# Linear attention and a routed expert layer on one core: early weights' low halves on VectorE, six PSUM banks for the early region, region 1's splits behind the rest's, eight groups

## The chip, the core and the metric

The kernel runs on one core of a Trainium2 chip. Each core has five engines that work side by side from their own instruction streams: TensorE (PE, with its weight loads as PEld), VectorE (DVE), ScalarE (ACT), GpSimd (POOL) and SyncE (SP), which here only issues transfers. They share SBUF, an on-chip memory of 128 partitions, and PSUM, in eight banks of which TensorE writes its results. An engine runs its instructions strictly in the order in which they were written. It waits on semaphores that other engines and transfers raise.

The metric is the time of one execution on the device in microseconds (us). Three runs of the kernel before took 570.96, 573.08 and 573.12 us (median 573.08). The profile was taken in an execution of 571.51 us, of which 569.8 us lie between the first and the last instruction; all times of steps below count from that first instruction.

A difference between two kernels is told as a ratio of their times with a 95% interval.

## What is computed

A linear attention feeds a mixture of 16 experts. Every token gets the one expert that two argmax choices pick, and its output is weighted by both softmax shares.

```python
kv  = einsum('bhsd,bhse->bhde', k, v)              # 8 batches, 8 heads, 576 tokens, 64 dims
out = einsum('bhsd,bhde->bhse', q, kv)
x   = out / sqrt(mean(out * out, -1) + 1e-6) * g_norm   # -> 4608 tokens x 512
g_idx = argmax(x @ w_group)                        # 4 groups
e_idx = argmax(x @ w_expert[g_idx])                # 4 experts of that group
h   = relu(x @ w1[g_idx, e_idx])                   # 512 -> 1024
y   = softmax_share_g * softmax_share_e * (h @ w2[g_idx, e_idx])   # 1024 -> 512
```

All inputs and the output are fp32. The expert products are made in three terms: a number is split into a high part that the reduced format fp32r holds and a low part that is the rest, and high x high, high x low and low x high are added up in PSUM. So every weight half and every activation needs one instruction for its high part (ACT, `whi`, `hh`, `hhi`, `xh`) and one for its low part (`wlo`, `hl`, `hlo`, `xl`).

## The kernel before

**Stage 1, to about 125 us.** The attention's batches are read, multiplied and normalised in 36 tiles of 128 tokens. The tiles are taken in seven groups (`GS = [6, 5, 5, 4, 4, 6, 6]`). For each group VectorE works out the routing (maximum L717, exponentials L721, the chosen expert L736, the tokens' ranks by expert L769, their row numbers `keys` L789), and POOL puts each tile's rows at those numbers into a table in device memory (`put_rows`, L248). The order of all this is not written out. Each piece is a `step` with an engine, an estimated length, a rank and the steps it needs, and `give_out` lists them: on the engine that can start first it takes, of the steps that are ready, the one with the smallest rank. The ranks come from the tables `RANK`, `ROUTE`, `FOLD`, `LOADS`, `QLOADS`, `KVS`. A step's `take` and `give` count slots of a pool of 11 weight-sized buffers (`big`, tag `w8`).

**Early products.** The table's rows are sorted by expert into regions, the largest regions first. After group `EARLY = 4` the first 256 rows (`HEAD`) of one expert's region are already there. They are read (L271, `xq0`), turned (L1166) and multiplied by that expert's weights while the last groups are still being routed: layer 1 in plain fp32 in eight pieces of 128 columns (L321), each followed by its high part on ACT (`hhi` L1190) and its low part on VectorE (`hlo` L1194); layer 2 in three terms (L332, L333, L337) for three of its four quarters. The quarters are (row half, column half): (0,0), (1,0), (0,1). `early_bank` hands out PSUM, two banks in turn. `LOWS = 'GGDD'` puts the low parts of the first two weight quarters on POOL and those of the other two on VectorE (`split_low`, L232). The result goes to the buffer `yos`, which takes a slot of the pool.

**Handover.** From here on the order is as written in the code. SP reads region 0's remaining 128 rows (`read(0)`, L271) once all rows are put, then region 1's first weight half, region 1's 364 rows (`read(1)`, eight transfers, L268) and the other three weight halves (L205). TensorE does the fourth quarter of the early layer 2 (first `CUT = 3` pieces, then the turning of the 128 rows L1415, then the rest), the 128 rows' layer 1 (L1454, eight chunks of which are named `hf` 0 and 1), the turning of its result (`turn`, L1436) and its layer 2 (`rest_layer2`: L332, L333, L337). ACT makes `hr` (L1455) and the high parts `hT` (L1439), VectorE the low parts (L1440). POOL scatters `yos` into the output (L286) in two halves, with the scaling of region 1's rows (L293) between them.

Into this stretch fall region 1's own preparations: the splits of its first weight half in two quarters (`split_piece`: ACT L228, VectorE L232) and, four times, a block of its rows turned on VectorE (L283), split high on ACT (L1356) and low on VectorE (L1360).

**Regions 1 to 15** follow one another: layer 1 in eight pieces (TensorE L332, L333, L337; ACT `hh` L296; VectorE `hl` L297), layer 2, the way back to token order and the scatter (L1369), while the next region's weights are loaded and split. After that comes a short part for tokens over a region's capacity, which with these inputs has nothing to do.

Of the kernel before, what the change touches and what calls it, by code (L numbers as in the profile page):

```python
# [9 lines left out]
F32 = mybir.dt.float32  # L10
# [14 lines left out]
GS = [6, 5, 5, 4, 4, 6, 6]  # L25
XO = 20
XR = 18
QUICK = [0, 1, 2, 3, 4, 5, 6]
# [7 lines left out]
RANK = {'hl': 9.65, 'wh': 6.62, 'wd': 2136.43, 'ek': 25.19, 'o': 25.25, 'ok': -55.65, 'sq': 5942.05, 'red': 15.18, 'w': 4025.37, 'wl': 3910.86, 'wl2': 2990.79, 'xt': -40.19, 'xs': -2498.44, 'l1': -61.45, 'hs': -2328.8, 'l2': -1.69, 'lk': -39.03}  # L36
ROUTE = [30.82, 25.75, 32.74, 13.04, -1952.63, 21.42, -2905.74]
FOLD = [-322.89, 2985.26, -27.49, -32.52, -3125.23, -19.02, 8.4]
LOADS = [-10693.24, -8621.11, -104.17, -10.74, 24.09, 22.45, 18.56, 2987.32]
QLOADS = [-6674.02, -5.16, 6.84, 24.17, -12.07, 23.8, 24.74, 3747.92]  # L40
KVS = [-5947.45, 47.59, 752.46, 9.1, -13.16, 2244.94, -6.35, 6.78]
# [3 lines left out]
LOWS = 'GGDD'  # L45
FILL = 0.28
LG = 0.19
FQ = [0, 1, 2, 3, 4, 5, 6]
# [11 lines left out]
def tile_linattn_moe(ctx: ExitStack, tc: tile.TileContext, qm, qt, k, v, router, w1, w2, out):  # L60
# [304 lines left out]
    with ExitStack() as ph:  # L365
# [774 lines left out]
        def early_products(wt):  # L1140
# [35 lines left out]
            hs = []  # L1176
            for f_ in range(FC):
                def f(f_=f_):
                    if f_ == 0:
# [4 lines left out]
                s = step("PE", 1.75, r0 + RANK["l1"] + 0.1 * f_, x + [free.pop(0), wt[f_ // 4]], f,  # L1184
                         give=1 if f_ == FC - 1 else 0)
# [5 lines left out]
                s = step("A", 0.3, r0 + RANK["hs"] + 0.1 * f_, [s], f, take=2 if f_ == 0 else 0)  # L1191
# [4 lines left out]
                hs.append(step("D", 0.33, r0 + RANK["hl"] + 0.1 * f_, [s], f))  # L1196
# [3 lines left out]
            for p in range(4):  # L1200
                def f(p=p):
                    if p % 2 == 0:
                        st["ws"][2 + p // 2] = [st["ws"][2 + p // 2], None, None]
                    split_high(st["ws"][2 + p // 2], p % 2)
                s = step("A", 0.95, r0 + RANK["wh"] + 0.1 * p, [wt[2 + p // 2]], f, take=2 - 2 * (p % 2))
# [456 lines left out]
```

## Time and profile before

| | before |
|---|---|
| median of three runs | 573.08 us (570.96 to 573.12) |
| profiled execution | 571.51 us |
| its span, first to last instruction | 569.8 us |
| granted TensorE clock, mean | 0.990 |
| PE busy / DVE / ACT / POOL | 538.4 / 392.7 / 273.9 / 266.0 us |
| bytes moved, mean rate | 126.29 MB, 222 GB/s |
| early layer 2 begins (L332) | 125.46 us |
| region 0's last 128 rows, layer 1 begins (L1454) | 138.73 us |
| region 1's layer 1 begins (L332) | 164.98 us |
| region 1's first `hh` (L296) | 168.89 us |

How to read it: a row of the timeline has the start of a group of like instructions, the time that they span, engine, line, operation, output and inputs with their shapes, and how many there are. A bracket at the end has the engine's idle time just before, and what released it. A row of the windows has a stretch, its length, the busy time of each engine, the granted clock, the mean busy share of the 16 transfer engines, and GB/s.

### The profile page before, as it was taken

How to read it: one execution, taken by the hardware profiler on the slowest of the kernel's cores; microseconds unless marked ns; L12 is line 12 of the kernel's file. 1: busy time of each engine (PE TensorE's matmuls, PEld its weight loads, DVE VectorE, ACT ScalarE, POOL GpSimd, SP SyncE). 2: the span in 40 equal slices, each digit the busy share in tenths (PEclk: the TensorE clock that was granted, in tenths of full speed). 3: DMA queues.
4: the chain of work that ended last, by engine and by line, in shares of the span. 5: the costliest groups of instructions: out<-in, count | busy, mean ns of one | idle time of the engine just before them, and what ended most of it. 6: DMA issues, size and time to landing. Idle time of an engine off the chain costs nothing. (4 is left out here: it accounts for less than half of the span.)

```text
span 569.8 us, 11665 instructions
## 1 busy us (share of the span) xinstructions
PE 538.4 (94%) x4267; PEld 512.4 (90%) x4273; DVE 392.7 (69%) x813; ACT 273.9 (48%) x490; POOL 266.0 (47%) x278
## 2 busy tenths in 40 slices
PE   6899999879399999999999999999999999999995
PEld 3789888667189999999999999999999999999995
DVE  2249799781249787687768686778787777777760
ACT  0458777521245353444544545454545546555450
POOL 5003465662210273555555647383836537364271
PEclk9999999999889999999999999999999999999999
DMA  8999997928845738262847372837466473854010
GB/s 264 371 413 372 398 420 308 353 91 237 272 174 187 296 87 310 76 251 88 267 167 275 117 302 86 307 110 301 165 242 226 161 312 92 326 187 168 14 36 32
DMA packets 44462, 126.29 MB, mean 222 GB/s; under 512 B 6901, under 2 KB 26857, under 8 KB 33396
## 3 DMA queue, kind: packets, MB, share of 16 engines
q1 hardware_dynamic: 36468, 106.01, 51.6%
q0 software_dynamic: 7792, 19.48, 9.2%
q8 instruction: 34, 0.56, 0.4%
q10 hardware_dynamic: 144, 0.04, 0.1%
q14 instruction: 24, 0.20, 0.1%
HBM read 106.04 MB, written 20.58 MB: 222 GB/s over the span
## 5 line engine op out<-in xcount | busy, mean ns | idle before, releaser
L1369 POOL DMA_INDIRECT out_dram<-z,idx x141 | 168.1, 1192 | 167.3 <-DVE idx L1342 128.6
L332 PE MATMUL ps<-xh,whi 128*128 128x364 f32 (+14 forms) x480 | 144.1, 300 | 0.5 <-ACT xh L1356 0.5
L333 PE MATMUL ps<-xl,whi 128*128 128x364 f32 (+14 forms) x480 | 144.0, 300 | 0.4 <-DVE xl L1360 0.4
L337 PE MATMUL ps<-xh,wlo 128*128 128x364 f32 (+14 forms) x480 | 144.0, 300 | 0.0
L337 PE MATMUL psy<-hh,w2l 128*128 128x364 f32 (+13 forms) x448 | 135.1, 302 | 0.4 <-DVE w2l L310 0.4
L333 PE MATMUL psy<-hl,w2h 128*128 128x364 f32 (+13 forms) x448 | 135.5, 302 | 0.0
L332 PE MATMUL psy<-hh,w2h 128*128 128x364 f32 (+13 forms) x448 | 134.8, 301 | 0.0
L232 DVE TENSOR_TENSOR wlo<-wr,whi 128x1024 fp32r<-128x1024 f32 x62 | 94.8, 1530 | 39.0 <-ACT whi L228 22.8
L333 PEld LDWEIGHTS ps<-xl,whi 128*128 128x128 f32 x480 | 90.6, 189 | 0.9 <-DVE xl L1360 0.9
L332 PEld LDWEIGHTS ps<-xh,whi 128*128 128x128 f32 x480 | 90.6, 189 | 0.8 <-ACT xh L1356 0.8
L337 PEld LDWEIGHTS ps<-xh,wlo 128*128 128x128 f32 x480 | 90.5, 189 | 0.0
L296 ACT ACTIVATE hh<-ps 128x364 fp32r<-128x364 f32 (+14 forms) x120 | 50.6, 421 | 81.1 <-PE ps L337 79.6
L310 DVE TENSOR_TENSOR w2l<-wr,w2h 128x1024 fp32r<-128x1024 f32 x60 | 73.5, 1224 | 17.7 <-ACT w2h L306 17.5
L337 PEld LDWEIGHTS psy<-hh,w2l 128*128 128x128 f32 x448 | 84.5, 189 | 0.7 <-DVE w2l L310 0.7
L306 ACT CAST w2h<-wr 128x1024 fp32r<-128x1024 f32 x60 | 62.6, 1043 | 46.0 <-PE psy L333 46.0
L332 PEld LDWEIGHTS psy<-hh,w2h 128*128 128x128 f32 x448 | 84.5, 189 | 0.0
L333 PEld LDWEIGHTS psy<-hl,w2h 128*128 128x128 f32 x448 | 84.5, 189 | 0.0
L297 DVE SCALAR_TENSOR_TENSOR hl<-ps,hh 128x364 fp32r<-128x364 f32 (+14 forms) x120 | 55.6, 464 | 26.6 <-ACT hh L296 26.4
L248 POOL DMA_INDIRECT xs<-xo,keys x36 | 37.6, 1045 | 72.7 <-ACT y L683 42.2
L228 ACT CAST whi<-wr 128x1024 fp32r<-128x1024 f32 x64 | 66.3, 1037 | 4.2 <-PE ps L1454 3.1
L1356 ACT ACTIVATE xh<-xt,rw 128x364 fp32r<-128x364 f32 (+14 forms) x60 | 32.7, 545 | 70.7 <-DVE xt L283 70.7
L293 POOL TENSOR_TENSOR xq<-xq 128x1280 f32<-128x1280 f32 (+4 forms) x15 | 36.2, 2415 | 23.3 <-DMA xq<-xs 23.1
(272 smaller groups left out, 676.6 us busy)
## 6 DMA issues: line engine op xcount, KB each, us to landing
wr<-in_w_dram SPq DMA_DIRECT2D x64, 1024.0 KB
m_q<-in_qm_dram SPq DMA_DIRECT2D x8, 1024.0 KB
m_k<-in_k_dram SPq DMA_DIRECT2D x7, 1024.0 KB
m_v<-in_v_dram SPq DMA_DIRECT2D x7, 1024.0 KB
xq<-xs SPq DMA_DIRECT2D x24, 136.0 KB
xq<-xs SPq DMA_DIRECT2D x20, 153.0 KB
out_dram<-z,idx POOLq DMA_INDIRECT x141, 3.0
xq<-xs SPq DMA_DIRECT2D x8, 187.0 KB
```

The costliest lines, as they stand in the source:

```text
L228: nc.scalar.copy(out=hi, in_=w)
L232: eng.tensor_tensor(out=lo, in0=w, in1=hi.bitcast(F32), op=ALU.subtract)
L248: sc = nc.gpsimd.indirect_dma_start(out=xs, out_offset=bass.IndirectOffsetOnAxis(ap=keys[:, c:c + 1], axis=0), in_=x.rearrange("p i f -> p ...
L293: eng.tensor_tensor(out=part(x, n), in0=part(x, n), in1=factors(x, n), op=ALU.mult)
L296: nc.scalar.activation(out=hh, in_=ps, func=AF.Relu)
L297: nc.vector.scalar_tensor_tensor(out=hl, in0=ps, scalar=0.0, in1=hh.bitcast(F32), op0=ALU.max, op1=ALU.subtract)
L306: nc.scalar.copy(out=piece(hi, hf, i2), in_=halfpiece(wt[hf][0], i2))
L310: nc.vector.tensor_tensor(out=piece(lo, hf, i2), in0=halfpiece(wt[hf][0], i2), in1=piece(hi, hf, i2).bitcast(F32), op=ALU.subtract)
L332: nc.tensor.matmul(ps, lhsT=stat_h(c), rhs=mov_h(c), start=(c == 0), stop=False)
L333: nc.tensor.matmul(ps, lhsT=stat_h(c), rhs=mov_l(c), start=False, stop=False)
L337: nc.tensor.matmul(ps, lhsT=stat_l(d), rhs=mov_h(d), start=False, stop=(d == n - 1))
L1369: sc = nc.gpsimd.indirect_dma_start(out=out4, out_offset=bass.IndirectOffsetOnAxis(ap=idx[:, g:g + 1], axis=0), in_=z[:, g, :], in_offset= ...
```

## The change

Five things are changed.

1. The 36 tiles are taken in eight groups instead of seven, the last two of 4 and 2 tiles in place of 6, and all tables of ranks hold other numbers. Attention work and its loads keep their number and their sizes.
2. All four early low halves are made on VectorE, behind the last group's ranks (`kr`); `LOWS` is gone.
3. `early_bank` hands out six banks in turn: the two of before and the four of the attention's output (`ps_o`, two tiles of two banks).
4. The early layer 2 is made by passes: for (0,0) and (1,0) first all 16 high x high products, then the 16 of high weights with low activations, then the 16 of low weights; then the same for (0,1). It has 72 matmuls as before. Its result goes into the first half of the `xx` buffer, which is free by then, so that `yos` takes no slot.
5. In the handover SP reads region 1's rows ahead of its first weight half; each of the other three weight halves is issued behind a piece of TensorE's work; and the two splits of the first half stand behind the two `turn`s instead of ahead of the first.

```diff
-GS = [6, 5, 5, 4, 4, 6, 6]
+GS = [6, 5, 5, 4, 4, 6, 4, 2]
-RANK = {'hl': 9.65, 'wh': 6.62, 'wd': 2136.43, ...}
+RANK = {'hl': 36.17, 'wh': 5.91, 'wd': 107.42, ...}
...
-LOWS = 'GGDD'
...
             def early_bank(nm):
+                i = bank[0] % 6
                 bank[0] += 1
-                return (ps_k, ps_e)[(bank[0] - 1) % 2].tile([P, 512], F32, name=nm, tag=("psk", "pse")[(bank[0] - 1) % 2])
+                if i < 2:
+                    return (ps_k, ps_e)[i].tile([P, 512], F32, name=nm, tag=("psk", "pse")[i])
+                if i % 2 == 0:
+                    t["o"] = ps_o.tile([P, 2, 512], F32, name=nm, tag="pso")
+                return t["o"][:, i % 2]
-            free = [done["kk", B - 1], None]
+            free = [done["kk", B - 1], None] + [done["lk", NTL - 2 + i // 2] for i in range(4)]
...
-                s = step(LOWS[p], 1.4 if LOWS[p] == "D" else 2.3, r0 + RANK["wd"] + 0.1 * p, [s] + ([done["kr", len(groups) - 1]] if p > 1 else []),
-                         lambda p=p: split_low(st["ws"][2 + p // 2], p % 2, nc.vector if LOWS[p] == "D" else nc.gpsimd),
+                s = step("D", 1.24, r0 + RANK["wd"] + 0.1 * p, [s, done["kr", len(groups) - 1]],
+                         lambda p=p: split_low(st["ws"][2 + p // 2], p % 2, nc.vector),
...
-            for n, (j, hf) in enumerate(((0, 0), (1, 0), (0, 1))):
+            def passes(j, hf, x):
+                js = slice(j * P, (j + 1) * P)
+                h, w = (t["h"], t["h"], t["l"])[x], st["ws"][2 + hf][(1, 2, 1)[x]]
+                for c in range(FC):
+                    nc.tensor.matmul(t["l2", j, hf][:, 0:DM // 2], lhsT=h[:, c, js], rhs=w[:, c, :],
+                                     start=(x == 0 and c == 0), stop=(x == 1 and c == FC - 1))
+            at = {}
+            for n, (j, hf, x) in enumerate([(j, 0, x) for x in (0, 2, 1) for j in range(2)] + [(0, 1, x) for x in (0, 2, 1)]):
...
-                        st["ys"] = big.tile([P, 2, DM], F32, name="yos", tag="w8")
+                        st["ys"] = t["t"].rearrange("p (j m) -> p j m", j=2)
...
         read(0, at[0])
+        read(1, at[1])
         w1n = [half_layer(ev, 0, 0)]
-        read(1, at[1])
-        w1n.append(half_layer(ev, 0, 1))
-        w2n = load_layer(ev, 1)
...
-        split_piece(w1n, 0)
-        split_piece(w1n, 1)
         x1 = new_x()
         for hf in range(2):
             ps = ps_h.tile([P, 512], F32, name="ps")
             for c in range(KC):
                 if hf == 1 and c == 2:
                     turn(0)
+                    split_piece(w1n, 0)
+                    w1n.append(half_layer(ev, 0, 1))
                 nc.tensor.matmul(ps, lhsT=xT[:, c, :], rhs=w1c[hf][:, c, :], start=(c == 0), stop=(c == KC - 1))
             nc.scalar.activation(out=hr[:, hf * 512:(hf + 1) * 512], in_=ps, func=AF.Relu)
         rest = [ps_h.tile([P, 512], F32, name="ps")[:, 0:DM // 2] for hf in range(2)]
+        w2n = [half_layer(ev, 1, 0)]
         rest_layer2(0, 0, 4)
         turn(1)
+        split_piece(w1n, 1)
+        w2n.append(half_layer(ev, 1, 1))
         rest_layer2(1, 0, 4)
```

What this does to the order on the engines, at three places. A row is a line, an operation, its output and inputs, a shape, and how many of them follow one another. The line numbers after the change are mostly one lower up to the early products, and 17 to 20 higher in the handover.

VectorE before, from the row numbers of the remaining 128 rows (`ridx`) to region 1's first blocks (`wr_2037` is region 1's first weight half, `xq_2013` its rows):

```order
L1429 SCALAR_TENSOR_TENSOR ridx<-xq_2012,bad_2095 128x1
L232 TENSOR_TENSOR wlo<-wr_2037,whi 128x4x256 x2
L1440 TENSOR_TENSOR hT<-ps,hT 128x512 x2
L283 STREAM_TRANSPOSE xt<-xq_2013 128x384
L1360 SCALAR_TENSOR_TENSOR xl<-xt,rw,xh 128x364
```

The same place after the change (`wr_2094` is now that weight half, `xq_2062` the rows):

```order
L1446 SCALAR_TENSOR_TENSOR ridx<-xq_2061,bad_2138 128x1
L1457 TENSOR_TENSOR hT<-ps,hT 128x512
L231 TENSOR_TENSOR wlo<-wr_2094,whi 128x4x256
L1457 TENSOR_TENSOR hT<-ps,hT 128x512
L231 TENSOR_TENSOR wlo<-wr_2094,whi 128x4x256
L282 STREAM_TRANSPOSE xt<-xq_2062 128x384
L1379 SCALAR_TENSOR_TENSOR xl<-xt,rw,xh 128x364
```

Each of the two low parts `hT`, which stood behind both splits of the weight half, now stands ahead of one of them; the first split of the half is behind the first `hT`.

SP's transfers before, from the read of region 0's last 128 rows on:

```order
L271 DMA xq_2012<-xs 128x544
L205 DMA wr_2037<-in_w_dram 128x2048
L268 DMA xq_2013<-xs 32x11x136
L268 DMA xq_2013<-xs 12x136
...
L205 DMA wr_2047<-in_w_dram 128x2048
L205 DMA wr_2049<-in_w_dram 128x2048
L205 DMA wr_2051<-in_w_dram 128x2048
```

And after:

```order
L270 DMA xq_2061<-xs 128x544
L267 DMA xq_2062<-xs 32x11x136
L267 DMA xq_2062<-xs 12x136
...
L204 DMA wr_2094<-in_w_dram 128x2048
L204 DMA wr_2170<-in_w_dram 128x2048
L204 DMA wr_2177<-in_w_dram 128x2048
L204 DMA wr_2200<-in_w_dram 128x2048
```

Region 1's first weight half moved from ahead of its rows' eight transfers (the left-out rows are six more of the same kind) to behind them. The order of the other three halves is the same.

POOL before, around the last puts of rows (`xs<-xo,keys`):

```order
L868 COPY xo<-tok_125 128x4x4
L248 DMA xs<-xo,keys 81920x544
L232 TENSOR_TENSOR wlo<-wr_1720,whi 128x8x128
L868 COPY xo<-tok_125 128x4x4
L248 DMA xs<-xo,keys 81920x544
L232 TENSOR_TENSOR wlo<-wr_1720,whi 128x8x128
L248 DMA xs<-xo,keys 81920x544 x6
L1321 MEMSET xq_2012 128x136
```

And after:

```order
L867 COPY xo<-tok_125 128x4x4
L247 DMA xs<-xo,keys 81920x544
L867 COPY xo<-tok_125 128x4x4
L247 DMA xs<-xo,keys 81920x544 x2
L867 COPY xo<-tok_125 128x4x4
L247 DMA xs<-xo,keys 81920x544 x2
L867 COPY xo<-tok_125 128x4x4
L247 DMA xs<-xo,keys 81920x544
L1340 MEMSET xq_2061 128x136
```

The two splits of early weights are gone from POOL, and the last six puts, all of one group before, now belong to two groups: the two tiles of the last group come as the third and the fifth of the six.

More of the change, by code (lines that the diff above doesn't have):

```diff
@@ L1175, in early_products @@
                 free.append(x[-1])
-            hs = []
+            hs, hhs, whs = [], [], []
             for f_ in range(FC):
@@ L1183, in f @@
                     whole1(ps[:, 0:HEAD], st["ws"][f_ // 4][:, :, f_ % 4 * P:(f_ % 4 + 1) * P], t["x"])
-                s = step("PE", 1.75, r0 + RANK["l1"] + 0.1 * f_, x + [free.pop(0), wt[f_ // 4]], f,
-                         give=1 if f_ == FC - 1 else 0)
+                s = step("PE", 1.82, r0 + RANK["l1"] + 0.1 * f_, x + [free.pop(0), wt[f_ // 4], done["o", NTL - 1]], f)
                 def f(f_=f_):
@@ L1190, in f @@
                     nc.scalar.activation(out=t["h"][:, f_, :], in_=t["l1", f_][:, 0:HEAD], func=AF.Relu)
-                s = step("A", 0.3, r0 + RANK["hs"] + 0.1 * f_, [s], f, take=2 if f_ == 0 else 0)
+                s = step("A", 0.38, r0 + RANK["hs"] + 0.1 * f_, [s] + ([first] if f_ else []), f, take=2 if f_ == 0 else 0)
+                first = s if f_ == 0 else first
+                hhs.append(s)
                 def f(f_=f_):
@@ L1211, in early_products, with f @@
             st["h"] = t
-            for n, (j, hf) in enumerate(((0, 0), (1, 0), (0, 1))):
-                def f(j=j, hf=hf):
-                    t["l2", j, hf] = early_bank("l2")
-                    head_layer2(t["l2", j, hf][:, 0:DM // 2], j, hf)
-                s = step("PE", 2.9, r0 + RANK["l2"] + 0.1 * n, [free.pop(0)] + ready[2 * hf:2 * hf + 2] + hs, f)
-                def f(j=j, hf=hf, n=n):
-                    if n == 0:
-                        st["ys"] = big.tile([P, 2, DM], F32, name="yos", tag="w8")
+            def passes(j, hf, x):
[6 more added lines that the diff above has]
+            for n, (j, hf, x) in enumerate([(j, 0, x) for x in (0, 2, 1) for j in range(2)] + [(0, 1, x) for x in (0, 2, 1)]):
+                def f(j=j, hf=hf, x=x):
+                    if x == 0:
+                        t["l2", j, hf] = early_bank("l2")
+                    passes(j, hf, x)
+                ws = slice(2 * hf, 2 * hf + 2)
+                s = at[j, hf] = step("PE", 0.98, r0 + RANK["l2"] + 0.1 * n, [
+                    free.pop(0) if x == 0 else at[j, hf]] + (whs[ws] + hhs if x == 0 else hs if x == 2 else ready[ws]), f)
+                if x != 1:
+                    continue
+                def f(j=j, hf=hf):
+                    if (j, hf) == (0, 0):
+                        st["ys"] = t["t"].rearrange("p (j m) -> p j m", j=2)
                     nc.scalar.copy(out=st["ys"][:, j, hf * (DM // 2):(hf + 1) * (DM // 2)],
                                    in_=t["l2", j, hf][:, 0:DM // 2])
-                free.append(step("A", 0.37, r0 + RANK["hs"], [s], f, take=1 if n == 0 else 0))
+                free.append(step("A", 0.37, r0 + RANK["hs"], [s], f))
         def vector_steps():
```

21 lines of the change are left out of this document (11 added, 10 removed).

## The prediction

> **What bounds the kernel now.** I read the windows first, to see which engine is full in which stretch.
>
> ```profile
> 60.00:80.00 20.00, 19.13 (x262) 17.65 (x264) 16.66 (x75) 14.62 (x40) 10.78 (x18) 1.00 1.02 407
> 116.00:120.00 4.00, 1.91 (x14) 1.31 (x14) 3.76 (x12) 1.01 (x2) 1.55 (x1) 1.00 0.13 45
> 130.00:140.00 10.00, 8.96 (x68) 8.08 (x67) 1.73 (x11) 1.81 (x4) 1.41 (x4) 1.00 0.76 225
> 225.00:250.00 25.00, 25.00 (x164) 25.00 (x163) 17.64 (x38) 11.39 (x18) 15.07 (x13) 1.00 0.45 149
> ```
>
> Columns: stretch, length, busy PE, PEld, DVE, ACT, POOL, granted clock, DMA share, GB/s. In the attention (60 to 80) the transfers are full (share 1.02) and PE nearly so. In the regions (225 to 250) PE is busy 25.00 of 25.00 at full clock: nothing but PE's own work sets that pace, and none of it is changed. Between them PE has holes: 1.91 busy of 4 from 116 to 120. So the question is when region 1 starts; from its first `hh` to the end the length is fixed. PE's timeline shows the holes.
>
> ```profile
> 114.84 1.99 PE L321 MATMUL l<-xx,wr 128*128 128x256 f32 x8 [1.43 <-DVE hlo L1194]
> 118.34 0.33 PE L760 MATMUL rk<-ohs,ones_b 128*128 128x96 bf16 x6 [1.10 <-DVE ohs L748]
> 119.71 5.45 PE L321 MATMUL l<-xx,wr 128*128 128x256 f32 x24 [0.98 <-DVE hlo L1194]
> 125.46 0.39 PE L332 MATMUL l<-whi,hhi 128*128 128x256 f32 x1
> 136.47 0.63 PE L1415 MATMUL ps<-ident,xT 128*128 128x128 f32 x4 [1.04 <-issue]
> 138.73 5.31 PE L1454 MATMUL ps<-wr,xT 128*128 128x512 f32 x12
> 144.90 0.66 PE L1436 MATMUL ps<-ident,hr 128*128 128x128 f32 x4 [0.86 <-ACT hr L1455]
> 145.40 1.88 PE L1454 MATMUL ps<-wr,xT 128*128 128x512 f32 x4
> 147.23 0.28 PE L333 MATMUL ps<-wlo,hT 128*128 128x256 f32 x1
> 156.44 0.58 PE L337 MATMUL ps<-whi,hT 128*128 128x256 f32 x1 [8.93 <-DVE hT L1440]
> 164.98 0.33 PE L332 MATMUL ps<-xh,whi 128*128 128x364 f32 x1
> ```
>
> The large one is 8.93 us ahead of 156.44, put down to VectorE's `hT`. VectorE, POOL, ACT and SP say why that is late.
>
> ```profile
> 111.59 2.24 DVE L721 TENSOR_TENSOR ex<-lg,mx 128x120 f32<-128x120 f32 x1
> 114.70 3.00 DVE L736 TENSOR_TENSOR oh<-oh,fi 128x120 f32<-128x120 f32 x1
> 120.77 0.25 DVE L789 TENSOR_REDUCE keys<-kr 128x6 int32<-128x96 f32 x1
> 135.68 0.69 DVE L275 TENSOR_TENSOR xT<-xq 128x512 f32<-128x512 f32 x1 [0.63 <-DMA xq<-xs]
> 153.43 2.36 DVE L232 TENSOR_TENSOR wlo<-wr,whi 128x1024 fp32r<-128x1024 f32 x2 [16.15 <-DMA xq<-xs]
> 155.71 0.68 DVE L1440 TENSOR_TENSOR hT<-ps,hT 128x512 fp32r<-128x512 f32 x1
> 161.06 0.57 DVE L283 STREAM_TRANSPOSE xt<-xq 128x384 f32<-128x384 f32 x1
> ```
>
> ```profile
> 111.31 2.36 POOL L232 TENSOR_TENSOR wlo<-wr,whi 128x1024 fp32r<-128x1024 f32 x1
> 121.30 1.90 POOL L248 DMA_INDIRECT xs<-xo,keys  x1 [3.75 <-DVE n_bc L1044]
> 129.09 0.98 POOL L248 DMA_INDIRECT xs<-xo,keys  x1 [0.30 <-issue]
> 143.32 2.77 POOL L293 TENSOR_TENSOR xq<-xq 128x1536 f32<-128x1536 f32 x1 [7.30 <-DMA xq<-xs]
> 146.25 1.02 POOL L286 DMA_INDIRECT out_dram<-yos,sidx  x1 [0.16 <-ACT hT L1439]
> ```
>
> ```profile
> 142.36 1.99 ACT L228 CAST whi<-wr 128x1024 fp32r<-128x1024 f32 x2 [3.06 <-PE ps L1454]
> 145.60 0.59 ACT L1439 CAST hT<-ps 128x512 fp32r<-128x512 f32 x1 [0.75 <-PE ps L1436]
> 168.89 0.49 ACT L296 ACTIVATE hh<-ps 128x364 fp32r<-128x364 f32 x1
> ```
>
> ```profile
> 132.38 0.33 SPq L271 DMA_DIRECT2D xq<-xs  x1
> 132.98 0.33 SPq L205 DMA_DIRECT2D wr<-in_w_dram  x1
> 139.88 1.90 SPq L205 DMA_DIRECT2D wr<-in_w_dram  x3
> SPq L271 <- DMA xs<-xo,keys: 4.3, 1, 4.3
> ```
>
> The `hT` that PE wants had its inputs at 146.2 (145.60 + 0.59), but stands behind the two splits `wlo` on VectorE, and these start at 153.43. Their weights and high parts were ready at 144.4 (142.36 + 1.99). The row names a transfer `xq<-xs`, long done; what really ends the wait is the other thing in the split's list of waits: its output takes the pool slot of `yos`, and the second half of `yos` is scattered only at 146.25, behind POOL's scaling. So issue end 147.27 and the splits' start 153.43 bound the landing: 6.2 us. Only an inference; the order of waits supports it.
>
> The smaller holes come from VectorE. L721 and L736 took 2.24 and 3.00 us; in the group before they were the following.
>
> ```profile
> 95.90 0.28 DVE L721 TENSOR_TENSOR ex<-lg,mx 128x120 f32<-128x120 f32 x1
> 96.85 0.28 DVE L736 TENSOR_TENSOR oh<-oh,fi 128x120 f32<-128x120 f32 x1
> ```
>
> Both long ones run beside a split on POOL (111.31 to 113.67; a second, equal one follows 3.9 us later), and end when it ends.
>
> **The change part by part.** *Low halves on VectorE.* POOL's two splits of 2.36 us go. VectorE gets two more splits; one there costs 1.22 us, by this row.
>
> ```profile
> 121.12 1.22 DVE L232 TENSOR_TENSOR wlo<-wr,whi 128x1024 fp32r<-128x1024 f32 x1
> ```
>
> L721 and L736 lose 1.96 + 2.72 = 4.7 us, so `keys` of the last group, at 120.77 before, comes at about 116; two tiny groups in place of one add some dozen instructions of 0.2 us, narrower than those replaced: about 1 us against me, 117. The last group's splits come behind `keys`, so they delay only what follows.
>
> The Trainium skill, "SBUF — State Buffer", section "SBUF: two separate sides", says that VectorE and GpSimd share a port pair as an exclusive lock held for a whole instruction. Here it agrees (2.24 and 3.00 against 0.28). It also warns that VectorE's work can starve transfers that GpSimd issues, which speaks against this edit. By that rule alone each of four puts would wait out a whole split, 4 x 1.22 = 4.9 us, an estimate that would make the forecast 560.0 by the margin below.
>
> Rows show that size: puts took 1.90 (121.30) while VectorE made a split, 0.98 (129.09) without. Four splits beside four puts are at most 4 x 0.92 = 3.7 us, at least nothing. I take 2.
>
> *Six banks and passes.* PE waited 1.43 + 1.10 + 0.98 = 3.51 us in the early layer 1, for a bank or for VectorE. With six banks and the routing rows short again, all three go. The first pass needs neither `hlo` nor `wlo`, so the four splits on VectorE hide behind 32 matmuls of it. Against it I set 0.3: one more group's rank matmuls (a group's took 0.33 in the row at 118.34), and a bank pair that two pieces share. So layer 2 begins at 125.46 - 3.2 = 122.3. Bounds: 0 to 3.5. The 72 matmuls stay as long as they were.
>
> *The remaining rows.* SP's read at 132.38 waited 4.3 us for the puts, the last of which ended at 130.07 (129.09 + 0.98), 2.3 before. With `keys` at 117, the last put depends on it only by four puts at 1.28 apart (0.98 + 0.30): 117 + 5.1 = 122, plus 2 for stretched ones 124, read 126.4. It landed 3.3 us after issue before (135.68 - 132.38): 129.7. VectorE wants it at 135.05 - 3.2 = 131.85 (135.68 less the 0.63 that it idled), so it is hidden with 2.1 to spare and the 0.63 goes too. `L1454` then begins at 138.73 - 3.2 - 0.63 = **134.9**, 3.8 earlier.
>
> *The handover*, counted from that start s. Before, the first transposition of region 1 (L283) is at s + 22.33 (161.06 - 138.73). Now, in the new order:
> - PE: twelve chunks, s + 5.31, and `turn(0)` at once, since ACT has no splits ahead of `hr` any more (the 0.86 goes); 0.66.
> - ACT: `hT` 5.31 + 0.7 (145.60 - 144.90) to s + 6.6; the first split's high part 1.0 (1.99 / 2) to s + 7.6. PE's second half ends 1.9 after `turn(0)`, at s + 7.7, so `hr` is ready at s + 8.3.
> - PE: first 12 matmuls of layer 2 (0.12 each; 2.00 / 18 = 0.11 in the 162 to 164 row below) to s + 9.1, `turn(1)`, ACT `hT` s + 9.8 to 10.4, second high part to s + 11.4.
> - VectorE: `hT` low 0.68 to s + 11.1, second split 11.4 + 1.2 to s + 12.5, then the first transposition.
>
> So it stands at 134.9 + 12.5 = 147.4 instead of 161.06: 13.7 earlier, of which 9.85 are this part. The stall's work is gone, not moved: `yos` holds no slot, so the split waits for its weights alone. These are issued behind `read(1)` (eight transfers, 4 us of issuing in the 130s), at about 131, and before took at most 6.9 us (132.98, next weights 139.88): 137.9, wanted at s + 6.6 = 141.5. Read(1) now comes before them and its scaling of 2.77 ends by 142, also ahead of 147.4. What is late next is the pace of the four blocks: 161.06 to `hh` at 168.89 is 7.83 us, on VectorE and ACT, and it stays. First `hh` at **155.2** instead of 168.89. PE's rest of region 0 ends at about s + 14 = 149, so PE waits for the blocks; no gain is left in it.
>
> *Tables, eight groups.* Same loads and products; transfers are the bound, so 0, bounded by one 1 MB load at the rate of the 60 to 80 row: 1.05 MB / 407 GB/s = 2.6 us either way.
>
> *Sum:* 3.2 + 0.63 + 9.85 = 13.7. Span 569.8 - 13.7 = 556.1; execution 571.51 - 13.7 = 557.8. The median of the runs is 1.57 above the profiled one (573.08), so I predict **559.4**.
>
> **The rivals.** *B: the read of region 0's rows gates as before.* The puts are spread by VectorE's splits or `keys` doesn't come earlier. From a last put later than 126.3 (131.85 - 3.3 - 2.3) each us costs one; at worst the read stays at 132.38 and only the handover's 9.85 is gained: 573.08 - 9.85 = 563.2. For it: the 1.90 row; against: 2 us to spare after 2 for stretching.
>
> *C: the clock.* From about 149 to 155 PE has 12 matmuls in 6 us. Before, in the long stall, the following held.
>
> ```profile
> 150.00:152.00 2.00, 0.00 (x0) 0.00 (x0) 0.00 (x0) 0.00 (x0) 0.00 (x0) 0.96 1.19 238
> 152.00:154.00 2.00, 0.00 (x0) 0.00 (x0) 0.57 (x1) 0.00 (x0) 0.00 (x0) 0.50 0.83 202
> 162.00:164.00 2.00, 2.00 (x18) 2.00 (x18) 1.09 (x2) 0.85 (x2) 0.00 (x0) 0.98 0.00 0
> ```
>
> Columns as above; the clock stands third from the end. It fell to half some 4.4 us after PE's last matmul at 147.51, and came back near 162, 5.5 us after work began at 156.44. Region 1's first 5.5 us at half clock would cost 2.75: 562.2. Against it: PE now pauses some 1.5 us between blocks (7.83 / 4, less three matmuls), and in the 116 to 120 row it was 48% busy with pauses of 1.10 and 0.98 at clock 1.00. The Trainium skill's "TensorE: Matmul & The Clock Gate", "Part 1: The HAM clock gate", puts the fall after an idle window of about 3.4 us and asks for no longer gaps. By it nothing falls here; the trace's 4.4 and 5.5 are later than its figure.
>
> *D: slower; the stall returns on ACT.* The second half of `xx` (now the early result) is still scattered behind the scaling, and the high part of region 1's second weight half takes a slot of that tile. It stands on ACT right ahead of the first `hh`, at about 154. With read(1) landed by 138, scaling by 142, scatter by 142 + 1 + 6.2 = 149: 5 us to spare. From a landing after 154 each us costs one, and slower than before begins at 168, if read(1) takes 20 us more. That needs weights, rows and puts to crowd each other: the rows (1.1 MB) and the two weight halves (2.1 MB) from 127 on, at the 225 GB/s of the mixed row, have landed by 141. Slower than before begins at 3.2 MB / 41 us = 78 GB/s; at 70 it is 173 and the time 573.1 + 5 = 578.
>
> *E: it does not do what it says.* The new tables give back in the attention what the handover gains: five 1 MB loads of 2.6 us late are 13, no change, 573. Nothing in the rows speaks for it: transfers full in both orders.
>
> **How the numbers follow.** Forecast 0.60, B 0.20, C 0.12, D 0.04, E 0.04. The forecast's own range is 556.8 to 562 (2.6 for the tables either way). The range reaches to B and C and one load step below, with the median's own spread of about 1: 555 to 566. About 0.5% (2.9 us) is what a measurement of this kernel can tell from no change. Forecast, B, C are all beyond: faster 0.92; same 0.04 (E); slower 0.04 (D).
>
> **What would show it.** Right: no row of some 9 us ahead of `hT`'s PE user; VectorE's L720 and L735 near 0.28; no POOL split; layer 2 of the early region near 122.3; region 0's `L1454` successor at 134.9; the first region 1 transposition near 147.4; first `hh` near 155.2; from there to the end 400.9 (569.8 - 168.89) as before. Wrong: a wait of VectorE or PE for `xq<-xs` in the 130s (B), a clock of 0.5 after 150 (C), an ACT wait for a slot at 154 (D), early products beginning much later than 106 (E).

## The result, and the profile after

The changed kernel takes 558.95 us (median of four runs, 558.03 to 559.98) against 572.48 us (four runs, 570.96 to 573.12). The ratio is 0.9768, 95% interval 0.9739 to 0.9797. The forecast was 559.4, range 555 to 566. The profiled execution of after is the longest of its four, 559.98 us, span 558.3.

Four of the runs below were made on a chip on which the kernel before took 612 to 615 us; of these I compare stretches counted from the start of the early products, not totals. Where their code is that of after, the stretches are the same to 0.02 us (to early layer 2, 15.59 or 15.60).

VectorE and SP of after, in the rows that answer to those of before:

```profile
113.58 0.20 DVE L788 TENSOR_REDUCE keys<-kr 128x4 int32<-128x64 f32 x1
116.01 0.16 DVE L788 TENSOR_REDUCE keys<-kr 128x2 int32<-128x32 f32 x1
116.54 1.21 DVE L231 TENSOR_TENSOR wlo<-wr,whi 128x1024 fp32r<-128x1024 f32 x1
...
132.21 0.21 DVE L1415 MEMSET psy<- 128x32 f32 x4 [6.08 <-ACT xx L1240]
132.77 0.69 DVE L274 TENSOR_TENSOR xT<-xq 128x512 f32<-128x512 f32 x1 [0.35 <-DMA xq<-xs]
142.21 0.69 DVE L1457 TENSOR_TENSOR hT<-ps,hT 128x512 fp32r<-128x512 f32 x1 [7.84 <-ACT hT L1456]
143.16 1.23 DVE L231 TENSOR_TENSOR wlo<-wr,whi 128x1024 fp32r<-128x1024 f32 x1 [0.26 <-ACT whi L227]
146.74 1.23 DVE L231 TENSOR_TENSOR wlo<-wr,whi 128x1024 fp32r<-128x1024 f32 x1 [0.26 <-ACT whi L227]
147.88 0.57 DVE L282 STREAM_TRANSPOSE xt<-xq 128x384 f32<-128x384 f32 x1
```

```profile
128.94 0.33 SPq L270 DMA_DIRECT2D xq<-xs  x1
129.49 4.02 SPq L267 DMA_DIRECT2D xq<-xs  x8
133.70 9.94 SPq L204 DMA_DIRECT2D wr<-in_w_dram  x4
```

POOL's last puts of rows, of which those at 116.76, 118.92 and 123.37 run beside one of the splits that VectorE makes from 116.54, 118.70 and 123.12 on:

```profile
116.76 1.85 POOL L247 DMA_INDIRECT xs<-xo,keys  x1 [0.28 <-DVE junk L1026]
118.92 1.84 POOL L247 DMA_INDIRECT xs<-xo,keys  x1 [0.30 <-issue]
120.74 1.06 POOL L867 COPY xo<-tok 128x16 int32<-128x16 int32 x1
...
123.37 1.81 POOL L247 DMA_INDIRECT xs<-xo,keys  x1 [0.30 <-issue]
...
125.66 0.98 POOL L247 DMA_INDIRECT xs<-xo,keys  x1 [0.28 <-POOL xo L867]
```

The splits of region 1 wait 0.26 us for their high parts, where VectorE idled 16.15 us before, the last of it for a buffer, and the two `hT` are made as soon as ACT has given them. `keys` of the last group come at 116.01 instead of 120.77. PE shows the same:

```profile
107.04 5.34 PE L320 MATMUL l<-xx,wr 128*128 128x256 f32 x24
...
115.17 7.15 PE L320 MATMUL l<-xx,wr 128*128 128x256 f32 x32
...
122.63 2.38 PE L1222 MATMUL l<-whi,hhi 128*128 128x256 f32 x16
...
133.52 0.66 PE L1432 MATMUL ps<-ident,xT 128*128 128x128 f32 x4 [0.72 <-DVE xT L274]
135.81 5.31 PE L1471 MATMUL ps<-wr,xT 128*128 128x512 f32 x12
```

```profile
155.71 0.48 ACT L295 ACTIVATE hh<-ps 128x364 fp32r<-128x364 f32 x1
```

No hole is left between 107 and 131, one of 0.72 us at 133, and none of 9 us. The steps of the sum against what the two profiles show (the early products begin at 106.11 before, 107.04 after):

| stretch | before | after | gain | forecast |
|---|---|---|---|---|
| start to early products | 106.11 | 107.04 | -0.93 | 0 |
| to early layer 2 | 19.35 | 15.59 | 3.76 | 3.2 |
| to the last rows' layer 1 | 13.27 | 13.18 | 0.09 | 0.63 |
| to region 1's first transposition | 22.33 | 12.07 | 10.26 | 9.85 |
| to its first `hh` | 7.83 | 7.83 | 0.00 | 0 |
| to the end | 400.91 | 402.59 | -1.68 | 0 |
| span | 569.8 | 558.3 | 11.5 | 13.7 |

The first line is the attention's own variation: in the runs below on the faster chips, kernels with one and the same attention begin their early products between 105.38 and 107.04. The last line is new:

```profile
149.00:155.40 6.40, 4.08 (x16) 2.17 (x15) 3.85 (x7) 2.94 (x7) 0.25 (x1) 1.00 1.00 229
156.00:158.00 2.00, 2.00 (x8) 2.00 (x8) 2.00 (x1) 1.13 (x2) 2.00 (x2) 0.50 1.05 426
```

```profile
152.64 0.44 PE L331 MATMUL ps<-xh,whi 128*128 128x364 f32 x1 [0.53 <-ACT xh L1375]
153.28 0.43 PE L332 MATMUL ps<-xl,whi 128*128 128x364 f32 x1 [0.20 <-DVE xl L1379]
...
155.47 0.48 PE L331 MATMUL ps<-xh,whi 128*128 128x364 f32 x1
155.74 0.51 PE L332 MATMUL ps<-xl,whi 128*128 128x364 f32 x1
159.00 0.33 PE L331 MATMUL ps<-xh,whi 128*128 128x364 f32 x1
```

PE's clock (third number from the end of a window) is at half from 155.5 to about 159, after 6 us in which PE had only 12 matmuls. That is rival C, beside the forecast rather than in its place.

### The profile page after: what moved, and what is told of

It reads as the page before. It is cut to its first block, busy times and chain, and to the rows that moved or that the text cites. A ratio compares the mean times of both kernels' runs of the same rounds, so it can differ in the third digit from the quotient of the medians.

```text
span 558.3 us, 11711 instructions
## 1 busy us (share of the span) xinstructions
PE 538.1 (96%) x4277; PEld 512.0 (92%) x4277; DVE 389.0 (70%) x838; ACT 273.7 (49%) x493; POOL 263.4 (47%) x280
## 5 line engine op out<-in xcount | busy, mean ns | idle before, releaser
L231 DVE TENSOR_TENSOR wlo<-wr,whi 128x1024 fp32r<-128x1024 f32 x64 | 97.0, 1516 | 23.6 <-ACT whi L227 23.6
L1563 DVE STREAM_TRANSPOSE z<-psy 128x320 f32<-128x320 f32 (+3 forms) x56 | 28.6, 510 | 24.1 <-PE psy L336 24.0
```

Of the source, the lines that this page charges most:

```text
L231: eng.tensor_tensor(out=lo, in0=w, in1=hi.bitcast(F32), op=ALU.subtract)
```

## The experiments

"L1 to hh" below is the time from the early products' start to region 1's first `hh`: 62.78 before, 48.67 after. "hh to end" is the rest of the span: 400.91 and 402.59.

**1. Which edit takes the long wait away?** The prediction said that `yos` holds no slot any more. The rival is that the order in which buffers are asked for decides.

Before, with the early result in the `xx` buffer:

```diff
-                        st["ys"] = big.tile([P, 2, DM], F32, name="yos", tag="w8")
+                        st["ys"] = t["t"].rearrange("p (j m) -> p j m", j=2)
```

> The kernel before with one edit: the early result goes into the first half of the xx buffer and yos takes no slot of the pool; all orders, banks and the handover as before. Theory S (the prediction's words: it is the slot of yos that makes the split wait): the splits start when weights and high parts are there, about 144.5 instead of 153.4, PE's 8.9 us wait goes, the clock stays up, ratio to before about 0.983 (some 10 us faster). Rival O (it is the order in which buffers are asked for: the split's output is simply the next buffer after four weight loads, and gets whatever is freed last, now the xx buffer that the same scatter empties): the split still starts near 153.4, ratio 1.000 within 0.003.

Measured: 572.25 against 572.41 us, ratio 1.000 (0.9984 to 1.0016).

```profile
147.25 1.01 POOL L286 DMA_INDIRECT out_dram<-xx,sidx  x1 [0.16 <-ACT hr L1455]
```

```profile
154.75 2.36 DVE L232 TENSOR_TENSOR wlo<-wr,whi 128x1024 fp32r<-128x1024 f32 x2 [15.23 <-DMA xq<-xs]
```

The scatter now empties `xx`, and the split starts 6.5 us after that scatter's issue ends (6.2 before). Counted from the early products it starts at 47.6 us, before at 47.3. Theory S falls.

After, with a slot for `yos` again:

```diff
-                        st["ys"] = t["t"].rearrange("p (j m) -> p j m", j=2)
+                        st["ys"] = big.tile([P, 2, DM], F32, name="yos", tag="w8")
```

> The kernel after with one edit: the early result has a slot of its own again (yos), all else as after. Theory S: the 8 us wait of the split comes back, ratio to before about 0.992. Rival O: with the loads asked for behind the splits, the late slot falls to the second weight half's high part, which is wanted only near 154 and whose scatter has landed by 147; ratio as after, 0.977 within 0.003.

Measured: 559.94 us, ratio 0.9791 (0.9750 to 0.9832), L1 to hh 49.00: as after within its interval. By the trace every stretch up to region 1's first transposition is as long as in after. The next one, to the first `hh`, is 8.16 us instead of 7.83, as in all six runs in which the clock fell to half well ahead of that `hh` (here it reads 0.66 from 152 to 154, in after 1.00). The slot as such is worth nothing.

Before, with the three loads alone moved:

```diff
-        w1n.append(half_layer(ev, 0, 1))
-        w2n = load_layer(ev, 1)
...
                     turn(0)
+                    w1n.append(half_layer(ev, 0, 1))
...
+        w2n = [half_layer(ev, 1, 0)]
         rest_layer2(0, 0, 4)
         turn(1)
+        w2n.append(half_layer(ev, 1, 1))
```

> The kernel before with one edit: the loads of region 1's other three weight halves are asked for behind the two splits (at the places where the change puts them); the splits stay ahead of hT, yos keeps its slot, everything ahead of the handover is as before. Theory O (the order in which buffers are asked for is the whole of the 8.9 us wait): the splits run at 144 to 147, PE's long wait goes down to about 1 us, region 1's first hh comes near 159 to 160 instead of 168.89, ratio to before 0.983 to 0.985. Rival: the wait needs the new position of the splits too, or the loads asked for later come late themselves: ratio above 0.99.

Measured: 562.47 us, ratio 0.9835 (0.9802 to 0.9868). L1 to hh is 52.83, 9.95 less than before.

```profile
140.69 1.99 ACT L228 CAST whi<-wr 128x1024 fp32r<-128x1024 f32 x2
141.78 2.36 DVE L232 TENSOR_TENSOR wlo<-wr,whi 128x1024 fp32r<-128x1024 f32 x2 [3.00 <-ACT whi L228]
146.63 0.69 DVE L1438 TENSOR_TENSOR hT<-ps,hT 128x512 fp32r<-128x512 f32 x1 [2.50 <-ACT hT L1437]
```

The splits run at 141.78, ahead of `hT` as before, and nothing waits for them. So by the times the move of three lines that ask for buffers is worth some 70% of the whole change; by the order of the code the late slot now falls to a split that is wanted much later.

The 9.95 understates it. The early part, with the code of before, took 21.02 us to early layer 2 instead of 19.35, because TensorE's clock fell to half in it (mean 0.68 from 119.7 to 125, 1.00 in the profile of before). The 24 matmuls that took 5.45 us in that profile took 7.13 here:

```profile
119.73 7.13 PE L321 MATMUL l<-xx,wr 128*128 128x256 f32 x24 [0.98 <-DVE hlo L1194]
```

From early layer 2 to the first `hh` this run needs 31.81 us, before 43.43 and after 33.08. In this stretch the three moved lines bring all that the whole change brings, and 1.27 us more: behind the second `hT` the blocks follow at once, where in after the second split stands between.

After, with the handover of before (loads and splits where they were):

```diff
+        w1n = [half_layer(ev, 0, 0)]
         read(1, at[1])
-        w1n = [half_layer(ev, 0, 0)]
+        w1n.append(half_layer(ev, 0, 1))
+        w2n = load_layer(ev, 1)
...
+        split_piece(w1n, 0)
+        split_piece(w1n, 1)
         x1 = new_x()
```

> The kernel after with the handover of before: region 1's first weight half ahead of its rows, all weight loads asked for ahead of the splits, both splits ahead of hT; the early part (eight groups, tables, low halves on VectorE, six banks, passes, yos in xx) stays. Theory O: the first split's output is again the buffer that the scatter empties last, VectorE waits 6 to 9 us for it, PE 6 to 8, the clock falls; only the early part's 3.8 us remain, some of it lost again: ratio to before 0.990 to 0.996. Rival: the early part alone moves the scatter ahead of the splits: ratio below 0.985.

Measured: ratio 0.9865 (0.9782 to 0.9948), too wide to place it; the trace is clear. PE waits for `hT` again,

```profile
169.33 0.58 PE L336 MATMUL ps<-whi,hT 128*128 128x256 f32 x1 [8.82 <-DVE hT L1459]
```

and L1 to hh is 58.83, 3.95 less than before: 3.75 of it up to early layer 2, and only 0.20 from there on (43.23 against 43.43). So the early part's gain comes on top of the handover's and makes none of it. That 3.95 and the 9.95 above add up to 13.90, near the 14.11 of both together, is in part luck, since the 9.95 holds the loss by the clock.

After, with the splits ahead of the last rows' layer 1:

```diff
+        split_piece(w1n, 0)
+        split_piece(w1n, 1)
         x1 = new_x()
...
-                    split_piece(w1n, 0)
...
-        split_piece(w1n, 1)
```

> The kernel after with one edit: region 1's two splits stand ahead of region 0's layer 1 again, as before the change (ACT, VectorE), while the weight loads stay where the change put them. Theory V (the position of the splits ahead of hT on the in-order VectorE and ACT matters): ACT makes both high parts ahead of the first hr, PE waits 1 to 2 us for it, region 1's first hh comes 1 to 2 us later than in after, ratio 0.979 to 0.981. Rival O (only the late slot mattered): the splits run as soon as the first half has landed, in time that VectorE and ACT have idle, first hh within 0.5 us of after's or earlier, ratio 0.975 to 0.978.

Measured: 560.30 us, ratio 0.9809 (0.9772 to 0.9846), L1 to hh 49.69, 1.02 more than after.

```profile
142.17 0.66 PE L1453 MATMUL ps<-ident,hr 128*128 128x128 f32 x4 [1.97 <-ACT hr L1473]
```

```profile
139.63 1.99 ACT L227 CAST whi<-wr 128x1024 fp32r<-128x1024 f32 x2 [4.17 <-DMA wr<-in_w_dram]
```

PE waits 1.97 us for ACT, which makes both high parts first, and these wait 4.17 us for the weights, which the change loads behind region 1's rows. Part of it comes back, since VectorE splits earlier. Of the 1.02, 0.69 are up to the first transposition, and 0.33 go with the earlier fall of the clock. So with the change's order of loads the title's "splits behind the rest's" is worth about 0.7 us by the trace; the times alone don't separate it from after.

With the loads' order of before it looks worth nothing: in the run with the three loads alone moved, ACT's high parts, at 140.69, wait for no weights, and from the last rows' layer 1 to `hh` that run takes 18.75 us, after 19.90. By these two traces the handover's other edits cost 1.15 us. This is not shown by a run of its own: none has after with the first weight half loaded ahead of the rows and the splits first.

**2. The early part.** After, with two banks:

```diff
-                i = bank[0] % 6
+                i = bank[0] % 2
...
-            free = [done["kk", B - 1], None] + [done["lk", NTL - 2 + i // 2] for i in range(4)]
+            free = [done["kk", B - 1], None]
```

> The kernel after with two PSUM banks in turn for the early region instead of six; passes, tables, eight groups and handover as after. By the prediction's term (banks and short routing rows together fill 3.5 us of holes) PE waits for hlo of the piece before the last at each of the eight pieces of layer 1; early layer 2 begins 2 to 4 us later than 122.6, and since puts and read have about 2 us in hand the total is 2 to 3 us longer, ratio 0.981 to 0.983. Rival: the short routing rows alone fill the holes, early layer 2 within 0.7 us, ratio as after (0.977).

Measured: 562.60 us, ratio 0.9818 (0.9783 to 0.9853). Early layer 2 begins 17.19 us after the early products (15.59 in after), 1.6 later and not 2 to 4. L1 to hh is 51.08: 2.4 more than after, 2.1 of it up to the last rows' layer 1 and 0.33 with the earlier fall of the clock.

```profile
111.09 1.99 PE L320 MATMUL l<-xx,wr 128*128 128x256 f32 x8 [0.63 <-DVE hlo L1199]
...
118.34 3.74 PE L320 MATMUL l<-xx,wr 128*128 128x256 f32 x16 [0.38 <-DVE hlo L1199]
```

The holes return, many and short, each an `hlo` that a bank waits for.

After, with the first two low halves on POOL:

```diff
-                s = step("D", 1.24, r0 + RANK["wd"] + 0.1 * p, [s, done["kr", len(groups) - 1]],
-                         lambda p=p: split_low(st["ws"][2 + p // 2], p % 2, nc.vector),
+                s = step("GGDD"[p], 2.3 if p < 2 else 1.24, r0 + RANK["wd"] + 0.1 * p, [s] + ([done["kr", len(groups) - 1]] if p > 1 else []),
+                         lambda p=p: split_low(st["ws"][2 + p // 2], p % 2, nc.gpsimd if p < 2 else nc.vector),
```

> The kernel after with the first two early low halves on POOL again (the last two stay on VectorE behind the ranks). By the prediction's step: the routing rows L720 or L735 of the small last groups, or other rows of VectorE beside them, are stretched from 0.2 to 2 us and more, keys come 2 to 5 us later, and POOL's own 4.7 us stand ahead of the last puts, so that the read of region 0's rows issues 3 to 6 us later than 128.9 and region 1 as much: ratio 0.982 to 0.987. Rival: with the new order POOL has room for them and only a little is stretched: ratio as after (0.977), read within 1 us of 128.9.

Measured: ratio 0.9892 (0.9781 to 1.0003); by the trace the early layer 2 begins 19.10 us after the early products (15.59 in after), the read issues at 25.54 (21.90), and L1 to hh is 52.59, 3.9 more (0.33 of it with the earlier fall of the clock).

```profile
129.04 2.16 DVE L747 TENSOR_TENSOR ohs<-ohb,sign 128x64 bf16<-128x64 bf16 x1
131.13 2.36 DVE L725 SCALAR_TENSOR_TENSOR oh<-ex,desc 128x40 f32<-128x40 f32 x1
133.41 0.19 DVE L806 TENSOR_SCALAR se<-se 128x20 f32<-128x20 f32 x1
```

```profile
128.77 4.66 POOL L231 TENSOR_TENSOR wlo<-wr,whi 128x1024 fp32r<-128x1024 f32 x2 [0.77 <-ACT whi L227]
```

Beside POOL's two splits, rows of VectorE that take 0.19 to 0.22 us in after take 2.16 and 2.36; it is whichever row comes next, not L721 and L736 as such.

After, with seven groups and the old tables:

```diff
-GS = [6, 5, 5, 4, 4, 6, 4, 2]
+GS = [6, 5, 5, 4, 4, 6, 6]
-RANK = {'hl': 36.17, ...}
+RANK = {'hl': 9.65, ...}
...
```

> The kernel after with the seven groups and all rank tables of before; banks, passes, low halves on VectorE and the handover as after. The prediction's term: tables and groups are worth 0, within 2.6 us either way, so the ratio is 0.977 within 0.005, with early layer 2 beginning within 1 us of 122.6. Rival T: the tables and the two small last groups are what filled the early layer 1; with the old ones the last group's keys come near 118 to 121, PE keeps 2 to 3 us of holes, early layer 2 begins near 125, ratio 0.982.

Measured: 570.56 us, ratio 0.9966 (0.9947 to 0.9984). Nearly all of the gain is gone, but not where either theory looked: early layer 2 begins at 123.23.

```profile
128.02 0.33 DVE L859 TENSOR_TENSOR xo<-nwy,cw 128x48 f32<-128x48 f32 x2
```

```profile
129.13 0.97 POOL L247 DMA_INDIRECT xs<-xo,keys  x1 [14.33 <-issue]
```

```profile
142.82 1.12 PE L1432 MATMUL ps<-ident,xT 128*128 128x128 f32 x4 [9.41 <-DVE xT L274]
```

With the old ranks the last group's token weights (L859) come behind the four low halves that VectorE now makes, at 128.02; its six puts begin at 129.13, the read of region 0's rows is late, and PE waits 9.41 us for it. This is the gate of rival B, but from another cause than it named: `keys` are there at 118.01, and none of the six puts is long.

The same with one number changed, the last group's rank for its token weights:

```diff
-FOLD = [-322.89, 2985.26, -27.49, -32.52, -3125.23, -19.02, 8.4]
+FOLD = [-322.89, 2985.26, -27.49, -32.52, -3125.23, -19.02, -60.0]
```

> The kernel after with seven groups and the rank tables of before, but one number of them changed: the last group's rank for the weights of its tokens, 8.4 to -60, so that these come ahead of the low halves on ACT and VectorE. Theory L (what the old tables cost in the run with them alone was this one inversion: the last group's token weights at 128 and its six puts behind them): puts end near 127, the read issues near 129 to 130, ratio 0.976 to 0.980 as after. Rival G (two small last groups are needed): the puts of a group of six start 2 us later and end 2 to 3 us later, read near 131, ratio 0.981 to 0.984.

Measured: ratio 0.9836 (0.9769 to 0.9903). By the trace, early layer 2 15.08 us after the early products (15.59), the read at 24.21 (21.90), PE waits 3.14 us for `xT`, L1 to hh 51.92: 3.25 more than after, against 10.33 more with the old tables unmended. So about 7 of the old tables' 10.3 us were this one inversion, and 3.25 are left for the groups and the other ranks.

**3. What bounds it now.** After, with 18 idle matmuls of zeros between the blocks of region 1's first piece:

```diff
+                        for _ in range(4):
+                            nc.tensor.matmul(psy[0][:, 0:352], lhsT=ones_b, rhs=wide_b[:, 0:352], start=True, stop=True)
...
+                            for _ in range(2):
+                                nc.tensor.matmul(psy[0][:, 0:352], lhsT=ones_b, rhs=wide_b[:, 0:352], start=True, stop=True)
```

> The kernel after with 18 idle matmuls of 352 columns on zeros added on PE between the blocks of region 1's first piece (from 150 to 155), where PE is thinly used; they write to a bank that later work starts anew. Theory C (the clock falls to half near 155.5 because PE was only a third used for 6 us): the clock stays 1.00 from 155 to 160, the time from the first hh to the end goes from 402.6 back to 400.9 as before the change, ratio 0.974, 1.5 to 2 us under after. Rival: the fall has another cause (the burst of loads at 414 to 426 GB/s at that time): the clock still reads 0.5 at 156 to 158 and the ratio is after's, 0.977.

Measured: 556.75 us, ratio 0.9724 (0.9696 to 0.9751). hh to end is 400.94, L1 to hh 48.68 as in after.

```profile
148.00:153.60 5.60, 5.49 (x28) 2.96 (x29) 3.32 (x7) 2.71 (x6) 0.10 (x1) 1.00 0.78 188
154.00:156.00 2.00, 2.00 (x14) 2.00 (x13) 1.80 (x1) 1.48 (x3) 1.99 (x2) 1.00 1.00 414
156.00:158.00 2.00, 2.00 (x14) 2.00 (x13) 2.00 (x1) 1.41 (x2) 1.30 (x1) 1.00 1.01 367
```

The clock holds at 1.00 under the same burst of loads (414 GB/s), so it was PE's thin use.

After, with region 1's blocks in the gaps of VectorE and ACT:

```diff
             nc.scalar.activation(out=hr[:, hf * 512:(hf + 1) * 512], in_=ps, func=AF.Relu)
+            if hf == 0:
+                xt1 = [turned(1, c) for c in range(3)]
+                for c in range(2):
+                    split_high_x(x1[0], xt1[c], 1, c)
+                for c in range(2):
+                    split_low_x(x1, xt1[c], 1, c)
+            else:
+                split_high_x(x1[0], xt1[2], 1, 2)
+                xt1.append(turned(1, 3))
+                split_low_x(x1, xt1[2], 1, 2)
...
         turn(1)
+        split_high_x(x1[0], xt1[3], 1, 3)
+        split_low_x(x1, xt1[3], 1, 3)
         split_piece(w1n, 1)
...
-        for c in range(KC):
-            prep(1, x1, c)
```

> The kernel after with region 1's four blocks (turning, high and low part) put into the gaps that VectorE and ACT have in the handover: three turnings and two splits right behind the first hr, the rest around the second turn. Theory P (after the change the pace of these blocks, 1.75 us each and 7.8 us from the first turning to hh, sets region 1's start): PE goes from region 0's last matmul (149.3) straight on, first hh near 151.5 instead of 155.7, and PE has no thin stretch, so the clock holds: 4 + 1.7 us less, ratio 0.966 to 0.968. Rival: the blocks ahead of hT on VectorE and ACT hold up the turns and the splits as much as they save, ratio 0.975 to 0.98.

Measured: 553.78 us (553.11 to 554.37), ratio 0.9678 (0.9651 to 0.9705), 5.2 us under after. L1 to hh is 44.39 (48.67), hh to end 400.89.

```profile
138.57 1.50 DVE L282 STREAM_TRANSPOSE xt<-xq 128x384 f32<-128x384 f32 x3 [4.93 <-POOL xq L292]
```

```profile
146.00:152.00 6.00, 6.00 (x45) 6.00 (x44) 3.40 (x5) 3.45 (x6) 0.98 (x1) 1.00 1.06 256
```

PE is busy without a pause from region 0's rest into region 1. This version beats both kernels.

The same, with the last two early low halves behind the first pass of the early layer 2:

```diff
+                if n == 2:
+                    for p in range(2, 4):
+                        low(p, at[0, 0])
```

> The kernel of e6_prep_early with one more edit: the last two early low halves on VectorE wait for the first pass of the early layer 2, so that they come behind the routing chain (indices, row starts) and behind POOL's last puts; they are wanted only by the last pass, near 130. Theory W (the puts took 1.8 us instead of 1.0 because VectorE made a split beside each): the third of the long puts and the stretched copy go back to 1.0 and 0.2, the last put ends 1.5 to 1.7 us earlier (17.9 to 18.1 us after the early products begin, 19.6 in after), the read issues about as much earlier (20.2 instead of 21.9), VectorE's wait for the rows goes and PE's 0.71 us wait becomes about 0.35: ratio to before 0.0005 under e6_prep_early's 0.9678, which the times can't tell from none; the trace decides. Rival: the puts are slow for another reason (their place in the queue), nothing moves.

Measured: ratio 0.9622 (0.9573 to 0.9672), on the slower chip, so not to be set against the run before it. Of the last six puts those two beside a split still take 1.85 and 1.84 us, the others 0.98; the read issues 20.24 us after the early products, 1.66 earlier than in after. But L1 to hh is 44.40, as without the edit: PE still waits 0.72 us for `xT`.

```profile
149.01 0.69 DVE L274 TENSOR_TENSOR xT<-xq 128x512 f32<-128x512 f32 x1 [0.35 <-DMA xq<-xs]
149.75 0.66 PE L1438 MATMUL ps<-ident,xT 128*128 128x128 f32 x4 [0.72 <-issue]
```

With the read 1.66 us earlier VectorE's pause of 0.35 is the same, so what ends it isn't the read, though the row names it. So the puts were not gating in after. What sets `xT` is the row ahead of it on VectorE, four `MEMSET`s of PSUM (132.21 in after), which wait for ACT's copy of the last pass of early layer 2 (131.76 to 132.13); in this run too they start 0.08 us after that copy. The 0.35 behind them stands, as 0.34 to 0.42, in every run whose rows came in time; what it is stays open.

## Why the prediction was right, and where its steps were off

*The early layer 1 (3.2).* Right: 3.76. All three holes went, `keys` came at 116.01 (about 116, set at 117), and both causes were tested: up to the last rows' layer 1 POOL's splits cost 3.6 us, two banks 2.1. They overlap, so they don't add up. That the size fits is in part luck of the profile it was read from: in the two other profiles with this early part (result in `xx` alone, three loads alone moved) the clock fell to half in it, and early layer 2 began after 20.72 and 21.02 us instead of 19.35. Against these the gain is 5.1 and 5.4.

*The last rows' read (0.63).* The size was off: 0.09. The read issued at 128.94, not 126.4. The last put ended 10.6 us after `keys`, not 7. The first put that needs the last `keys` starts 2.9 us after them, at 118.92, behind a long put of the group before, which the forecast put at nothing. From there two long puts and a slow copy add 2.5 us to the four puts, where I took 2. It cost nothing all the same: the run with the earlier read kept PE's wait of 0.72. Nor was the whole 0.63 there to gain, since the pause behind the `MEMSET`s stays at 0.34 or more: VectorE's pause fell from 0.63 to 0.35, and PE's wait from 1.04 to 0.72. Against this stands the early layer 2 itself, 8.9 us from its first matmul to the first of the fourth quarter, 8.7 before, which the forecast had unchanged.

The Trainium skill, "SBUF — State Buffer", section "SBUF: two separate sides", warns of starved transfers for VectorE operations in its two-port modes; the forecast's sentence left this condition out. The puts here are long beside a subtraction of two SBUF inputs, 1.84 against 0.98, and the one whose subtraction was moved is short again; so in this trace such an operation delays puts as well. The estimate made from it, a whole split (1.22) for each of four puts, was above what was measured, 0.87 for each of three.

*The handover (9.85).* The size was right (10.26; its own terms give 22.33 - 12.5 = 9.83) and its schedule within half a us: first transposition at s + 12.07 (12.5), s being the start of the last rows' layer 1. The weights' 6.9 us was luck: the issue of the next weights, from which it was read, doesn't bound a landing, but in the run with the splits ahead ACT could use weights issued at 132.81 from 139.63 on, 6.8 us later. The reason given for the gain was wrong in one point. "`yos` holds no slot, so the split waits for its weights alone" fell with the first two runs: without its slot the wait stays, with its slot it stays away. It is the order in which buffers are asked for: before, four weight loads took the free ones, and the split's output got the one that a scatter empties last. Nor was the schedule the best one: the second split ahead of the blocks is what the run with the three loads alone does without. The chain of the wait itself (scaling, scatter, split, `hT`, PE) was as read.

*The pace of the blocks (7.83).* Right, and named as what is late next; to the hundredth by luck, since it is 8.15 or 8.16 where the clock falls sooner. Taking it away was worth 4.3 us and, with it, the clock.

*The tables (0, within 2.6).* For the attention it held. But the term left out that the new order of work on VectorE needs new ranks: the old ones cost 10.3 us, by the gate of rival B.

*Rival C* had its price (2.75 forecast, 1.68 measured) but not its exclusion: I held pauses to be short enough because they were shorter than in the row at 116 to 120. There PE was 48% busy in the 4 us, and in the 6.3 us from 113.4 it had at most 2.80 us of work. After, from 149 to 155.4, its twelve matmuls of 0.167 us are 2 us of work in 6.4. The busy time of that window, 4.08, counts waiting matmuls. And the row was one execution: the same stretch of the same code did bring the clock to half in two other profiles, so it was no evidence that such pauses are safe.

*Rivals D and E* did not come: ACT's high part of the second weight half ran at 154.76 without a wait.

The median's gain of 13.5 against a sum of 13.7 is in part luck. In the profiled pair the three steps gave 14.11, less 0.93 by the attention's spread and 1.68 by the clock, which is 11.5; and the profile of before is one of those without a fall of the clock in the early part.

## What to carry to other kernels

A pool of buffers can make waits by the order in which its tiles are asked for: here the split that asked after four early loads got the buffer that came free last, and its in-order engine passed the wait on to all that stood behind it. So ask for buffers in the order in which their contents are wanted, and look, for every long wait, at all that the waiting instruction waits for, since the row names only one thing. When work moves to another engine in a listed schedule, its rank there has to be chosen anew. Where PE is left with thin work for some us, put preparations into earlier gaps, or keep it busy, even where one profile shows the full clock: the next execution may not.

## What the runs showed of the hardware

The clock fell without a pause of PE longer than 0.53 us by its rows: 12 matmuls in 6.4 us (a third of the time) brought it to half for 3.5 us, and 18 idle matmuls in the same stretch held it. The early layer 1 of before is such a stretch as well: PE had at most 2.80 us of work in 6.3 (44%), with pauses up to 1.65 us. With the same code there, the profile of before keeps 1.00, while in the runs with the result in `xx` alone and with the three loads alone moved the clock was at half for some 3 us from 120 on, and 24 matmuls took 6.86 and 7.13 us instead of 5.45. No run here gives a share of use that is safe.

On the faster chips hh to end was 401.9 to 403.1 in all runs with that thin stretch, and 400.9 in those without it (before, with the result in `xx` alone, filled, blocks early). The Trainium skill's "TensorE: Matmul & The Clock Gate", "Part 1: The HAM clock gate", names an idle window of about 3.4 us; no window of that length was idle here by the rows, so by these traces a thinly used one can be enough.
